# A planned two-layer kernel: seven products for eight in one more pair, and a planner with issue intervals

## The chip, the cores and the metric

The kernel runs on one core of a Trainium2 chip. The metric is the device time of one launch in microseconds: 1023.86 us, the median of three runs (1023.51 to 1023.94). TensorE (PE) does the matmuls, VectorE (DVE) and ScalarE (ACT) everything between them, SyncE (SP) issues nearly all transfers; GpSimd (POOL) does next to nothing. Each engine works through its own list in the order in which the program gives it.

## The reference

From q, k and v of 6016 tokens by 256 channels the reference makes a channel attention, and then two feed-forward layers on 6016 tokens with 2048 hidden features:

```
qn = q / (norm(q over tokens) + 1e-6);  kn likewise
a  = softmax(kn^T @ qn / tau);  x = v @ a              # 6016 x 256
x  = (max(x @ w_in, 0) ** 2) @ w_out                   # layer 1
h  = x @ moe2_w_in
y  = max(0.01 * h, h) @ moe2_w_out                     # layer 2
```

The weights arrive as 64-bit floats and are converted in the kernel.

## The kernel before, in words

A short attention stage (to about 52 us) makes the 256 x 256 softmax, which is folded into layer 1's w_in. Then come the two layers. The tokens are cut into six pairs of two blocks of 512 tokens (448 in pair 4); pairs are counted from 0 in each layer, and a layer's eight groups of 256 hidden features (g = 0 to 7) from 0 too. A unit is one pair and one group, so there are 96 units. Layer 1's pair 0 has a fixed order of its own (PLAIN, line 532); the other 88 units are laid out by a planner.

Every fp32 product is three matmuls on split operands: each operand is a high part and a low part, and mm3 (line 555) adds low x high, high x high and high x low into one bank. "A cast" on ACT makes the high part, "a low" on DVE (line 116) subtracts it to give the low part.

In a unit the first product (x @ w_in) is a 2 x 2 block product done with seven block products in place of eight: F1, F2, F3, F5, F4, F7, F6 in this order (line 907), each three matmuls into two banks. Banks are ha and hb, or hc and he in every second unit of a plain pair. After F1 ACT copies the bank away (C11, line 1317), after F3 it makes copy u, after F4 copy w; DVE adds F2's, F5's and F6's bank to these copies (lines 564 and 566), and F7 is read by ACT (line 1331). F6 may start only when DVE has added F5's bank to copy w. Then ACT squares (layer 1) or applies the leaky relu, casts, and DVE makes the lows.

The second product (g @ w_out) of a unit is either plain, eight block products (line 583, form "P"), or shared, seven products P1 to P7 (line 645, form "S"). Before, form S is used in layer 2's pairs 0 to 4 for the groups SG = 0, 1, 3, 4, 6 (lines 55 and 550). A pair with such groups is called mixed: its units all use banks ha and hb, bank c gathers P1, P6 and P7 (yA in the profile) and bank e gathers P5 (yF). A form-S unit needs four subtractions on DVE (lines 1420 to 1423), three more casts and lows (b), and weight sums S1 to S4 of w_out; the gathered banks are added up by take_shared and combine (lines 1470 and 1547).

Layer 2's weights are converted in 16 steps (Unit, line 130, and convert, line 978) during layer 1's pairs 2 to 5, spread evenly (line 1593).

The planner (line 751 on) makes a list of tasks with an engine, a cost, a due time, dependencies and buffers; one unit of time is a 512-column matmul. simulate (line 804) lets each engine take the ready task with the smallest due time; a result can be used on another engine lat = 0.3 after the task's end. TensorE takes the next first product, or a second product that waits in a list, with small gaps (PE, line 859). The due times are written by hand relative to the unit's start. The plan is made eight times, each on the unit starts of the one before, and the last is used. A function deadlines (line 1621) that works times back from the matmuls stands in the file, but late_start stays None and nothing calls it.

Of the kernel before, what the change touches and what calls it, by code (L numbers as in the profile page):

```python
# [18 lines left out]
P = 128  # L19
# [12 lines left out]
def attn_moe_moe2(  # L32
# [22 lines left out]
    SG = (0, 1, 3, 4, 6)  # L55
# [30 lines left out]
    def bank(tag, name):  # L86
# [43 lines left out]
    class Unit:  # L130


        def __init__(self, kind, L, g):
            self.kind, self.L, self.g = kind, L, g
            self.blocks = L == 2 and (kind == "i" or g in SG)

# [614 lines left out]
    tasks, lines = [], {}  # L751
    COST = {"v": 10, "out": 9, "y": 5, "wi": 2.6, "wo": 1.6, "wst": 2, "store": 2, "x": 1.6}
# [51 lines left out]
    def simulate(pe):  # L804
# [16 lines left out]
        while n:  # L821
# [31 lines left out]
    TURNS = 8  # L853
    LOAD = 22
# [74 lines left out]
    def batch_of(n):  # L929
        i = sorted(SG).index(units[n][2])  # L930
        return i // BATCH, i % BATCH
# [6 lines left out]
    def is_mixed(L, p):  # L938
        return L == 2 and p < NP - 1 and len(SG) > 0
# [6 lines left out]
    def build(base):  # L946
# [31 lines left out]
        def convert(u, due, loaded=None, first=None, pace=4, begin=0):  # L978
# [16 lines left out]
            re = T("ACT", 2.7, d(0.5), u.rebias, deps=[t], uses=[ce])  # L995
# [43 lines left out]
        for n in range(NG):  # L1039
# [3 lines left out]
            if g + 1 < NG:  # L1043
# [7 lines left out]
                lo = [T("DVE", 2.5, at0(m["fold_low"] + 2.6 * i), lambda i=i, pw=pw: fold_low(i, *pw[i]), deps=[hi[i]], uses=[b])  # L1051
                      for i in range(KC)]
# [6 lines left out]
            for i, (half, fb) in enumerate(((0, 0), (0, 1), (1, 0), (1, 1))):  # L1059
# [9 lines left out]
                relus[half, fb] = T("ACT", 2.7, at0(m["relu"][i]), plain_relu, n, half, fb, deps=[t], **k)  # L1069
# [63 lines left out]
        def prepare_x(L, p):  # L1133
# [34 lines left out]
            else:  # L1168
# [4 lines left out]
                t = T("SP", "x", t0 + 30, load, alloc=xr, lat=2.5 * LOAD, deps=[stores["y", 1, p, 0], stores["y", 1, p, 1]])  # L1173
# [83 lines left out]

        def load_wo(n):
            L, p, g = units[n]
            b = wo_b[L, p, g] = Buf("wo", 4, base[n] + 13)  # L1260
            dep = stores["o", L, g]
            if form_of(n) == "P":
                def load():
                    src = wo_d[L, g]
                    if L == 2 and g in SG:
                        src = src[:, :, :4].rearrange("p a (k b) m -> p a k b m", k=KC)
                    nc.sync.dma_start(raw(wo_tile(L, p, g)), src)

                wo_ready[L, p, g] = T("SP", "wo", base[n] + 13, load, alloc=b, lat=LOAD, deps=[dep])
                return  # L1270

            def load():
                t = wo_t[L, p, g] = wpool.tile([P, 2, 4, P], F32R, tag="wo", name="wo", bufs=4)
                nc.sync.dma_start(raw(t), wo_d[L, g][:, :, 1:5])

            def load_s1():
                t = late_w[n, "S1"] = wpool.tile([P, 2, 1, P], F32R, tag="ws", name="ws", bufs=2)
                nc.sync.dma_start(raw(t), wo_d[L, g][:, :, 5:6])

            def load_s23():  # L1280
                t = late_w[n, "S23"] = cpool.tile([P, 2, 2, P], F32R, tag="ce", name="ws")
                nc.sync.dma_start(raw(t), wo_d[L, g][:, :, 6:])
# [187 lines left out]
        def take_shared(p, which, b, after):  # L1470
            w = WIDTH[p]
            s = (w + 32) / 544
            n = (NP + p) * NG
            due = base[n] + (b + 1) * 4 * 42
            a = lambda: y_t[2, p, "A"][:, :w]

            def new():
                if which == "P1":
                    sum_t[p, "P1"] = cpool.tile([P, 512], F32, tag="cm", name="acc")
                elif which == "U":  # L1480
                    t = vpool.tile([P, 2, 512], F32, tag="v", name="acc")
                    sum_t[p, "U"], sum_t[p, "V"] = t[:, 0], t[:, 1]
                nc.scalar.copy(sum_t[p, which][:, :w], a())

            def more():
                add(sum_t[p, which][:, :w], sum_t[p, which][:, :w], a())

            due += {"P1": 0, "U": 30, "V": 45}[which]
            if b == 0:
                if which == "P1":  # L1490
                    sums_b[p, "P1"] = Buf("cm", 2, due)
                elif which == "U":
                    sums_b[p, "U"] = sums_b[p, "V"] = Buf("v", 3, due)
                k = dict(uses=[sums_b[p, which]]) if which == "V" else dict(alloc=sums_b[p, which])
                t = T("ACT", 2.7 * s, due - 20, new, deps=after + ([got["U"]] if which == "V" else []), **k)
            else:
                t = T("DVE", 3 * s, due - 20, more, deps=after + [got[which]], uses=[sums_b[p, which]])
# [5 lines left out]
        def mixed_items(n):  # L1503
            L, p, g = units[n]
            gs = sorted(SG)
            prev = n - 1 if g - 1 in SG else None
# [12 lines left out]
            else:  # L1519
# [5 lines left out]
                if ends:  # L1525
                    members = [m for m in range(n - g, n) if units[m][2] in SG and batch_of(m)[0] == b]
                    take_shared(p, "P1", b, list(in_batch))
                    in_batch.clear()
                    for which, acc, mine in (("P6", "U", own[:3]), ("P7", "V", own[3:])):
# [3 lines left out]
                        take_shared(p, acc, b, xs)  # L1533
# [10 lines left out]
            if g == NG - 1:  # L1544
                combine(p)

        def combine(p):
            w = WIDTH[p]
            s = (w + 32) / 544
            y = lambda half, d: y_t[2, p, half, d][:, :w]  # L1550
            S = lambda which: sum_t[p, which][:, :w]
            f = lambda: y_t[2, p, "F"][:, :w]
            t0 = base[(NP + p + 1) * NG]
            D1 = 3 * s
            B = sums_b
            Y = lambda half, d: done[2, p, half, d]

            def x_new():
                sum_t[p, "X"] = cpool.tile([P, 512], F32, tag="cm", name="acc")
                add(S("X"), S("V"), y(0, 0))  # L1560

            y11 = T("DVE", D1, t0 + 40, lambda: add(S("P1"), S("P1"), y(0, 1)), deps=[got["P1"], *Y(0, 1)], uses=[B[p, "P1"]])
            B[p, "X"] = Buf("cm", 2, t0 + 45)
            y21 = T("DVE", D1, t0 + 45, x_new, deps=[got["V"], *Y(0, 0)], alloc=B[p, "X"], uses=[B[p, "V"]])
            fu = T("DVE", D1, t0 + 42, lambda: add(S("U"), S("U"), f()), deps=[got["U"], *f_done], uses=[B[p, "U"]])
# [104 lines left out]
```

## Time and profile before

| | |
|---|---|
| Median of runs | 1023.86 us (1023.51 to 1023.94) |
| Profiled execution | 1023.25 us |
| Span of the profile | 1021.5 us |
| TensorE busy | 1016.0 us (99%), 4693 matmuls |
| Weight loads (PEld) busy | 859.1 us (84%) |
| VectorE busy | 793.8 us (78%), 1131 instructions |
| ScalarE busy | 765.8 us (75%), 1170 instructions |
| Mean granted TensorE clock | 0.999 |
| Moved by DMA | 215.95 MB, 211 GB/s |

The profile is one execution; 1.75 us of its time lie outside the span. Matmuls overlap, so a group's duration is longer than the distance between starts, and the distance is what counts. In the table by stretches each pair of layers 1 and 2 is one stretch, from the pair's first first-product to the next pair's.

### The profile page before, as it was taken

The numbers are of one execution on the slowest core, as the hardware profiler recorded it, in microseconds if no ns is written. First come the engines' busy times: TensorE is split into PE (matmuls) and PEld (weight loads), VectorE is DVE, ScalarE is ACT, GpSimd is POOL, SyncE is SP. The second block draws the span as 40 slices with busy tenths as digits, with TensorE's granted clock in tenths as the row PEclk, the third lists the DMA queues.
The fourth block names the chain that finished last, engine by engine and source line by source line (L and its number), as shares of the span: only waits on it lengthen the run. The fifth ranks groups of instructions, "written<-read, shape, count | busy, mean of one in ns | idle before, by whom it ended". The sixth has DMA issues, their size and how long they took to land.

```text
span 1021.5 us, 13002 instructions
## 1 busy us (share of the span) xinstructions
PE 1016.0 (99%) x4693; PEld 859.1 (84%) x4693; DVE 793.8 (78%) x1131; ACT 765.8 (75%) x1170; POOL 0.7 (0%) x6
## 2 busy tenths in 40 slices
PE   9999999999999999999999999999999999999998
PEld 8888888888888888998888888888888888898887
DVE  5999878967976977888747779979979979977442
ACT  6798777877877877888767778778777777775662
POOL 0000000000000000000000000000000000000000
PEclk9999999999999999999999999999999999999999
DMA  9795568568678667787735555755755654664521
GB/s 350 278 233 179 165 209 245 177 220 256 235 255 271 226 249 235 270 292 274 271 135 189 197 191 191 221 200 178 220 190 200 199 197 173 199 232 157 173 78 42
DMA packets 125600, 215.95 MB, mean 211 GB/s; under 512 B 49376, under 2 KB 65760, under 8 KB 123232
## 3 DMA queue, kind: packets, MB, share of 16 engines
q1 hardware_dynamic: 124816, 214.46, 62.8%
q8 instruction: 37, 0.61, 0.2%
q10 hardware_dynamic: 720, 0.66, 0.2%
q14 instruction: 27, 0.22, 0.1%
HBM read 174.98 MB, written 40.11 MB: 211 GB/s over the span
## 4 chain that ended last, share of the span: by engine, by line
PE 99%; ACT 0%; DVE 0%; issue 0%
PE y L557 40%; PE ha L557 17%; PE hb L557 13%; PE hc L557 6%; PE yA L557 5%; PE he L557 5%; PE h L714 4%; PE sT L399 4%; PE y L597 2%; PE yF L557 2%; PE pw L265 1%; PE warm L364 0%; ACT e L486 0%; PE pn L373 0%; ACT whl L205 0%; DVE cm L178 0%
## 5 line engine op out<-in xcount | busy, mean ns | idle before, releaser
L557 PE MATMUL y<-g,wo 128*128 128x512 f32 (+1 forms) x1758 | 448.6, 385 | 0.0
L557 PEld LDWEIGHTS y<-g,wo 128*128 128x128 f32 x1758 | 329.8, 188 | 62.1
L116 DVE TENSOR_TENSOR g<-c,g 128x1024 fp32r<-128x1024 f32 (+1 forms) x192 | 229.4, 1200 | 80.3 <-ACT g L684 59.4
L557 PE MATMUL ha<-x,wi 128*128 128x512 f32 (+1 forms) x768 | 212.7, 385 | 0.0
L557 PEld LDWEIGHTS ha<-x,wi 128*128 128x128 f32 x768 | 143.7, 188 | 27.3 <-ACT c L1317 0.5
L557 PE MATMUL hb<-x,wi 128*128 128x512 f32 (+1 forms) x576 | 159.6, 385 | 0.0
L684 ACT CAST g<-c 128x1024 fp32r<-128x1024 f32 (+1 forms) x142 | 145.8, 1034 | 13.2 <-PE y L557 7.6
L557 PEld LDWEIGHTS hb<-x,wi 128*128 128x128 f32 x576 | 107.6, 188 | 20.8 <-ACT c L1324 0.4
L699 ACT ACTIVATE c<-c 128x512 f32<-128x512 f32 (+1 forms) x160 | 98.5, 621 | 18.4 <-DVE c L564 16.1
L557 PE MATMUL hc<-x,wi 128*128 128x512 f32 (+1 forms) x288 | 80.1, 386 | 0.0
L701 ACT ACTIVATE c<-c 128x512 f32<-128x512 f32 (+1 forms) x98 | 60.8, 621 | 12.8 <-DVE c L566 12.1
L1412 DVE TENSOR_TENSOR c<-c 128x512 f32<-128x512 f32 (+1 forms) x100 | 67.7, 677 | 3.1 <-ACT c L701 0.6
L1317 ACT COPY w<-ha 128x512 f32<-128x512 f32 (+1 forms) x64 | 37.0, 578 | 43.7 <-PE ha L557 43.3
L557 PEld LDWEIGHTS hc<-x,wi 128*128 128x128 f32 x288 | 53.7, 188 | 10.6 <-ACT c L1317 0.8
L557 PE MATMUL he<-x,wi 128*128 128x512 f32 (+1 forms) x216 | 60.2, 387 | 0.0
L1390 ACT CAST g<-c 128x1024 fp32r<-128x1024 f32 (+1 forms) x50 | 51.3, 1025 | 4.7 <-DVE c L1412 3.3
L116 DVE TENSOR_TENSOR b<-c,b 128x512 fp32r<-128x512 f32 (+1 forms) x75 | 49.5, 673 | 2.9 <-ACT b L1405 2.3
L1405 ACT CAST b<-c 128x512 fp32r<-128x512 f32 (+1 forms) x75 | 44.5, 610 | 5.7 <-PE yA L557 2.4
L714 PE MATMUL h<-x,wi 128*128 128x512 f32 x192 | 47.9, 391 | 0.0
L116 DVE TENSOR_TENSOR x<-xr,x 128x1024 fp32r<-128x1024 f32 (+3 forms) x44 | 46.9, 1066 | 1.1 <-ACT x L1188 1.0
L557 PEld LDWEIGHTS he<-x,wi 128*128 128x128 f32 x216 | 40.1, 188 | 7.7 <-DVE c L564 0.6
L1317 ACT COPY u<-ha 128x512 f32<-128x512 f32 (+1 forms) x64 | 36.9, 576 | 12.5 <-PE ha L557 9.7
(134 smaller groups left out, 1170.7 us busy)
## 6 DMA issues: line engine op xcount, KB each, us to landing
wi<-wi SPq DMA_DIRECT2D x80, 896.0 KB, 5.1
wo<-wo SPq DMA_DIRECT2D x96, 512.0 KB, 4.7
wi<-wi SPq DMA_DIRECT2D x24, 512.0 KB, 4.1
wst<-in_moe_w_in_dram SPq DMA_DIRECT2D x16, 512.0 KB, 6.4
wst<-in_moe_w_out_dram SPq DMA_DIRECT2D x16, 512.0 KB, 5.7
wi<-wis SPq DMA_DIRECT2D x8, 1024.0 KB, 5.3
ws<-wo SPq DMA_DIRECT2D x25, 256.0 KB, 3.1
x<-o SPq DMA_DIRECT2D x20, 256.0 KB, 5.5
```

What stands on the lines that cost most here:

```text
L116: tt(lo, x, raw(hi), op=ALU.subtract)
L399: nc.tensor.matmul(sT[j][:, :C], t[:, 0, i, j * P : (j + 1) * P], t[:, 1, i], start=n == 0 and i == 0, stop=last_tile and i == g - 1,)
L557: nc.tensor.matmul(ps, a[m], b[n], start=first and i == 0, stop=i == 2, skip_group_check=True)
L597: nc.tensor.matmul(y_bank(L, p, 1, t // 2)[:, t % 2 * C : (t % 2 + 1) * C], gt[:, a, fb, t * P : (t + 1) * P], wo[:, b, :, fb], start=(g, ...
L684: nc.scalar.copy(g_t[n, half][:, 0, :, :w], c)
L699: nc.scalar.activation(c, c, AF.Square)
L701: nc.scalar.activation(c, c, AF.Prelu, alpha=0.01)
L714: nc.tensor.matmul(h_t[n, half, fb][:, :w], a[i], b[j], start=start, stop=stop, skip_group_check=True)
L1317: nc.scalar.copy(to, h(0))
L1390: nc.scalar.copy(g_t[n, name][:, 0, :, :w], result(n, half, w))
L1405: nc.scalar.copy(b_t[n, name][:, 0, :w], c(half, fb))
L1412: tt(c(*to), c(*a), c(*b), op=ALU.subtract)
```

## The change

Form S is no longer tied to layer 2. A table GROUPS gives the groups for each layer and pair: layer 1's pair 5 gets 0, 1, 3, 4, 6, and layer 2's pairs 0 to 4 get 0, 2, 3, 4, 6 where they had 0, 1, 3, 4, 6. For layer 1 the weight sums of w_out are made once: in pair 4, when a group's plain weights are loaded, wo_sums joins high and low, makes the four sums, splits them and stores them to wo_s, from which pair 5 loads. combine for layer 1 stores the four sums to x2 straight from its accumulators. Layer 2's conversions are spread over pairs 2 to 4 (CONV_BEGIN, CONV_END).

The planner changes too. A task's cost on DVE and ACT is now the distance to the next start, 0.37 and 0.45 less than before, and its result comes 0.6 and 0.65 after that; a result of TensorE comes 0.95 after its cost, before 0.3. From the third plan on, tasks of DVE and ACT are ordered by deadlines(), worked back from the matmuls that need them, and of the plans from the third on the one whose TensorE ends first is used.

```diff
-    SG = (0, 1, 3, 4, 6)
+    GROUPS = {(1, 5): (0, 1, 3, 4, 6), **{(2, p): (0, 2, 3, 4, 6) for p in range(5)}}
+    SG = {L: sorted({g for (l, _), x in GROUPS.items() if l == L for g in x}) for L in (1, 2)}
...
-        return "S" if L == 2 and p < NP - 1 and g in SG else "P"
+        return "S" if g in GROUPS.get((L, p), ()) else "P"
...
+    PIPE = {"DVE": (0.37, 0.6), "ACT": (0.45, 0.65), "PE": (0, 0.95), "POOL": (0, 0.6)}
...
+            else:
+                less, lat = PIPE[engine]
+                cost -= less
...
-        known = {t: sorted((b.due, b.due + 30) for b in lines.get(t, ())) for t in free_lines}
+        known = {t: sorted((b.due, b.due + 60) for b in lines.get(t, ())) for t in free_lines}
...
+    FIRST_MIXED = min([p for L, p in GROUPS if L == 1], default=0)
+    CONV_BEGIN, CONV_END = 2, 5
...
+        def wo_sums(n, ready, b):
...
+            def join():
+                r["x"] = cpool.tile([P, 8, P], F32, tag="whl", name="wr")
+                r["s"] = out_sums(r["x"])
+                hi, lo = (raw(wo_t[L, p, g][:, m]).rearrange("p k b m -> p (k b) m") for m in range(2))
+                tt(r["x"][:, :4], hi, lo, op=ALU.add)
...
+            t = T("DVE", 3, e, join, deps=[ready], alloc=xb, uses=[b])
+            for i in range(4):
+                t = T("DVE", 1.1, e + 1, lambda i=i: r["s"][i](), deps=[t], uses=[xb])
+            wb = Buf("wis", 1, e + 6)
+            t = T("ACT", 4.6, e + 6, high, deps=[t], alloc=wb, uses=[xb])
+            t = T("DVE", 5.2, e + 12, lows, deps=[t], uses=[xb, wb])
+            stores["o", 1, g, "s"] = T("SP", "store", e + 20, store, deps=[t], uses=[wb])
...
+                if L == 1 and g in SG[1] and p == FIRST_MIXED - 1:
+                    wo_sums(n, wo_ready[L, p, g], b)
...
+                if L == 1:
+                    for which, d, dep in parts:
+
+                        def put_sum(which=which, d=d, half=half):
+                            nc.sync.dma_start(x2_d[p][:, SLOT[d, half], :w], S(which))
...
-                span = base[6 * NG] - 60 - base[2 * NG]
+                begin = base[int(CONV_BEGIN * NG)] + 60
+                span = base[int(CONV_END * NG)] - 60 - begin
...
+        if turn >= 2 and (best is None or free["PE"] < best[0] - 0.05):
+            best = free["PE"], list(tasks), dict(c_tag)
+        if turn >= 1:
+            late_start = deadlines()
+    tasks[:] = best[1]
```

How the order moves is seen at two places. On TensorE, in layer 1's pair 5 before, one unit (x_3434, x_3885, x_3803 and x_3792 are the four tiles of the pair's x; F1, F2, F3, F5, F4, F7, F6 are the ha and hb rows, in this order, and the y rows are second products):

```order
L557 MATMUL ha<-x_3434,wi 128x512 x3
L557 MATMUL hb<-x_3792,wi 128x512 x3
L557 MATMUL y<-g,wo 128x512 x3
L557 MATMUL ha<-x_3885,wi 128x512 x3
L557 MATMUL y<-g,wo 128x512 x3
L557 MATMUL hb<-x_3803,wi 128x512 x3
L557 MATMUL ha<-x_3803,wi 128x512 x3
L557 MATMUL y<-g,wo 128x512 x6
L557 MATMUL ha<-x_3885,wi 128x512 x3
L557 MATMUL hb<-x_3792,wi 128x512 x3
L557 MATMUL y<-g,wo 128x512 x12
```

The same pair on TensorE now, one unit (x_3493, x_3965, x_3906, x_3899 are the same four tiles):

```order
L559 MATMUL ha<-x_3493,wi 128x512 x3
L559 MATMUL hb<-x_3899,wi 128x512 x3
L559 MATMUL y<-g,wo 128x512 x3
L559 MATMUL ha<-x_3965,wi 128x512 x3
L559 MATMUL y<-b,wo 128x512 x3
L559 MATMUL hb<-x_3906,wi 128x512 x3
L559 MATMUL yF<-g,ws 128x512 x3
L559 MATMUL ha<-x_3906,wi 128x512 x3
L559 MATMUL y<-g,wo 128x512 x3
L559 MATMUL yF<-g,ws 128x512 x3
L559 MATMUL ha<-x_3965,wi 128x512 x3
L559 MATMUL hb<-x_3899,wi 128x512 x3
```

Products of the shared form (y<-b, yF, and yA outside these rows) stand among the first products; from F4 (the third ha row) to F6 (the last hb row) there are nine matmuls in both.

On VectorE, the start of layer 1's pair 5 before (c<-c,hb and the like are the adds on the banks, g<-c,g are lows; ce, cm and wr belong to the conversion of layer 2's weights):

```order
L564 ISA c<-c,hb 128x512
L116 TENSOR_TENSOR g<-c,g 128x2x448
L149 TENSOR_SCALAR ce<-wst 128x512
L156 TENSOR_SCALAR cm<-wst 128x512
L159 SCALAR_TENSOR_TENSOR cm<-wst,cm 128x512
L162 SCALAR_TENSOR_TENSOR ce<-wst,ce 128x512
L564 ISA c<-w,hb 128x512
L174 SCALAR_TENSOR_TENSOR wr<-cm,ce 128x256 x2
L220 TENSOR_TENSOR wr<-wr 128x128
L221 TENSOR_TENSOR wr<-wr 128x128
L564 ISA c<-u,hb 128x512
```

VectorE at that place now (L1456 c<-c are the four subtractions of a shared unit, b<-c,b its lows):

```order
L566 ISA c<-w,hb 128x512
L566 ISA c<-u,hb 128x512
L118 TENSOR_TENSOR g<-c,g 128x1024
L1456 TENSOR_TENSOR c<-c 128x512
L566 ISA c<-c,hb 128x512
L118 TENSOR_TENSOR b<-c,b 128x512
L1456 TENSOR_TENSOR c<-c 128x512 x3
L118 TENSOR_TENSOR b<-c,b 128x512 x2
L566 ISA c<-w,hb 128x512
L750 COPY o<-y 128x448
L118 TENSOR_TENSOR g<-c,g 128x1024
```

The conversion's rows have left the pair, and the subtractions and extra lows of the shared form have come.

## Rows read from the trace of the kernel before

**Rows 1.** The page: busy time by engine, and the chain that ended last.
```profile
PE 1016.0 (99%) x4693; PEld 859.1 (84%) x4693; DVE 793.8 (78%) x1131; ACT 765.8 (75%) x1170; POOL 0.7 (0%) x6
...
PE 99%; ACT 0%; DVE 0%; issue 0%
```

**Rows 2.** Timeline of TensorE, 560 to 568 us: start, duration, instructions, count.
```profile
560.80 0.84 PE L557 MATMUL hb<-x,wi 128*128 128x512 f32 x3
...
567.60 0.85 PE L557 MATMUL y<-g,wo 128*128 128x512 f32 x3
```

**Rows 3.** Stretches (layer 1's pairs 0, 2 to 5; layer 2's pair 0): busy us.
```profile
60.00:143.00 83.00, 83.00 (x401) 69.99 (x400) 75.98 (x126) 68.81 (x101) 0.00 (x0) 1.00 0.65 200
...
220.50:302.70 82.20, 82.20 (x362) 67.32 (x362) 65.12 (x97) 64.41 (x95) 0.00 (x0) 1.00 0.75 251
302.70:384.50 81.80, 81.80 (x362) 67.23 (x361) 61.12 (x92) 62.16 (x94) 0.00 (x0) 1.00 0.74 250
384.50:459.00 74.50, 74.50 (x362) 67.33 (x361) 61.34 (x92) 59.32 (x97) 0.00 (x0) 1.00 0.78 269
459.00:539.70 80.70, 80.70 (x362) 67.55 (x361) 55.35 (x77) 61.41 (x93) 0.00 (x0) 1.00 0.61 222
539.70:617.30 77.60, 77.60 (x344) 64.21 (x343) 57.98 (x75) 59.20 (x94) 0.00 (x0) 1.00 0.54 192
```

**Rows 4.** Waits of TensorE's weight loads: total us, times, longest us.
```profile
PEld hc L557 <- ACT c L1317: 0.8, 4, 0.2
PEld he L557 <- DVE c L564: 0.6, 3, 0.3
PEld ha L557 <- ACT c L1317: 0.5, 2, 0.3
```

**Rows 5.** Timeline, 882 to 884 us (PEld is the weight load).
```profile
882.06 0.77 PE L557 MATMUL hb<-x,wi 128*128 128x448 f32 x3
...
882.67 0.77 PE L557 MATMUL ha<-x,wi 128*128 128x448 f32 x3
...
882.87 0.55 ACT L1324 ACTIVATE c<-hb 128x448 f32<-128x448 f32 x1 [0.39 <-PE hb L557]
...
883.47 0.50 PEld L557 LDWEIGHTS hb<-x,wi 128*128 128x128 f32 x3 [0.40 <-ACT c L1324]
883.47 0.87 PE L557 MATMUL hb<-x,wi 128*128 128x448 f32 x3
```

**Rows 6.** Groups of VectorE by line and shape: count, busy us, mean ns, idle before.
```profile
L116 DVE TENSOR_TENSOR g<-c,g 128x1024 fp32r<-128x1024 f32 x160 | 194.7, 1222 | 68.0 <-ACT g L684 51.1 <-ACT g L1390 15.8
L1412 DVE TENSOR_TENSOR c<-c 128x512 f32<-128x512 f32 x80 | 55.2, 690 | 2.0
L116 DVE TENSOR_TENSOR b<-c,b 128x512 fp32r<-128x512 f32 x60 | 40.6, 687 | 2.7 <-ACT b L1405 2.3
...
L116 DVE TENSOR_TENSOR wis<-wr,wis 128x1024 fp32r<-128x1024 f32 x13 | 15.8, 1217 | 0.3 <-ACT wis L205 0.3
...
L220 DVE TENSOR_TENSOR wr<-wr 128x128 f32<-128x128 f32 x21 | 6.0, 288 | 0.3
...
L1230 DVE TENSOR_TENSOR wr<-wi 128x512 f32<-128x512 f32 x8 | 5.5, 685 | 0.0
```

**Rows 7.** Groups of ScalarE by line and shape.
```profile
L1405 ACT CAST b<-c 128x512 fp32r<-128x512 f32 x60 | 36.3, 621 | 4.8 <-PE yA L557 2.1 <-PE y L557 0.8 <-ACT c L701 0.3
...
L1317 ACT COPY w<-ha 128x512 f32<-128x512 f32 x52 | 30.6, 588 | 38.8 <-PE ha L557 38.7
```

**Rows 8.** The page's DMA issues: count, KB each, median us to landing.
```profile
wi<-wi SPq DMA_DIRECT2D x80, 896.0 KB, 5.1
```

**Rows 9.** Timeline of VectorE, 862.7 to 864 us.
```profile
862.69 0.62 DVE L566 TENSOR_TENSOR c<-u,hb 128x448 f32<-128x448 f32 x1 [1.16 <-PE hb L557]
863.26 1.09 DVE L116 TENSOR_TENSOR g<-c,g 128x896 fp32r<-128x896 f32 x1
```

**Rows 10.** Waits of all engines: total us, times, longest us.
```profile
DVE c L564 <- ACT w L1317: 27.4, 24, 3.1
```

More of the change, by code (lines that the diff above doesn't have):

```diff
@@ L134, in __init__ @@
             self.kind, self.L, self.g = kind, L, g
-            self.blocks = L == 2 and (kind == "i" or g in SG)
+            self.blocks = L == 2 and (kind == "i" or g in SG[2])
         def load(self):
@@ L938, in is_mixed @@
     def is_mixed(L, p):
-        return L == 2 and p < NP - 1 and len(SG) > 0
+        return len(GROUPS.get((L, p), ())) > 0
     c_tag = {}
@@ L1260, in load_wo @@
             b = wo_b[L, p, g] = Buf("wo", 4, base[n] + 13)
-            dep = stores["o", L, g]
+            dep = stores["o", L, g] if L == 2 or form_of(n) == "P" else stores["o", 1, g, "s"]
+            sums_d = wo_d[L, g] if L == 2 else wo_s.get(g)
             if form_of(n) == "P":
@@ L1490, in take_shared @@
                 if which == "P1":
[L1491 removed]
+                    sums_b[L, p, "P1"] = Buf("cm", 2, due)
                 elif which == "U":
[L1493 to L1494 removed]
+                    sums_b[L, p, "U"] = sums_b[L, p, "V"] = Buf("v", 3, due)
+                k = dict(uses=[sums_b[L, p, which]]) if which == "V" else dict(alloc=sums_b[L, p, which])
                 t = T("ACT", 2.7 * s, due - 20, new, deps=after + ([got["U"]] if which == "V" else []), **k)
             else:
[L1497 removed]
+                t = T("DVE", 3 * s, due - 20, more, deps=after + [got[which]], uses=[sums_b[L, p, which]])
             got[which] = t
@@ L1525, in mixed_items @@
                 if ends:
-                    members = [m for m in range(n - g, n) if units[m][2] in SG and batch_of(m)[0] == b]
-                    take_shared(p, "P1", b, list(in_batch))
+                    members = [m for m in range(n - g, n) if units[m][2] in gs and batch_of(m)[0] == b]
+                    take_shared(L, p, "P1", b, list(in_batch))
                     in_batch.clear()
@@ L1554, in combine @@
             D1 = 3 * s
             B = sums_b
-            Y = lambda half, d: done[2, p, half, d]
+            Y = lambda half, d: done[L, p, half, d]
             def x_new():
-                sum_t[p, "X"] = cpool.tile([P, 512], F32, tag="cm", name="acc")
+                sum_t[L, p, "X"] = cpool.tile([P, 512], F32, tag="cm", name="acc")
                 add(S("X"), S("V"), y(0, 0))
-            y11 = T("DVE", D1, t0 + 40, lambda: add(S("P1"), S("P1"), y(0, 1)), deps=[got["P1"], *Y(0, 1)], uses=[B[p, "P1"]])
@@ L1569, in combine @@
+            fv = T("DVE", D1, t0 + 50, lambda: add(S("V"), S("V"), f()), deps=[got["V"], y21, *f_done], uses=[B[L, p, "V"]])
+            y12 = T("DVE", D1, t0 + 53, lambda: add(S("U"), S("U"), y(1, 1)), deps=[fu, *Y(1, 1)], uses=[B[L, p, "U"]])
+            y22 = T("DVE", D1, t0 + 56, lambda: add(S("V"), S("V"), y(1, 0)), deps=[fv, *Y(1, 0)], uses=[B[L, p, "V"]])
             F_after[0] = [fu, fv]
-            if p == NP - 2:
+            q = (L, p + 1) if p < NP - 1 else (2, 0)
+            if not is_mixed(*q):
```

95 lines of the change are left out of this document (56 added, 39 removed).

## The prediction

> **What bounds the kernel now.** I read the engine table and the chain of waits first, then the table by stretches cut at the pairs, then TensorE's timeline, then its waits. TensorE is busy 1016.0 of 1021.5 us and the chain that ended last is TensorE for 99% [rows 1]. Busy time of a pipelined engine proves little, so the issue rate has to be looked at: in the first mixed pair of layer 2 ten groups of three matmuls start between 560.80 and 567.60 us, 30 matmuls in 6.80 us, or 0.2267 us each, without one skipped beat [rows 2]. Cut at the pairs, TensorE fills every stretch, while VectorE fills 69 to 92% of it and never runs out [rows 3]. So the time is the number of matmuls times their issue interval, plus the places where a weight load had to wait. After the first fold those places are few: three groups of waits with nine places and 1.9 us [rows 4], and a tenth place of 0.40 us [rows 5], 2.3 us together. Not all of that reaches the matmuls. At that tenth, at 883.47 us, the weight load waited 0.40 us for ScalarE; the matmul group before began at 882.67 and, at the 0.61 us that a group of 448 columns took just before (882.06 to 882.67), the next was due at 883.28 and began at 883.47, so 0.19 us was lost [rows 5]. Half of 2.3 us, about 1.1 us, is my estimate of all that better ordering could still give back there.
>
> **The matmuls removed.** In the last pair of layer 1 (pair 5; a layer's pairs count from 0) five of eight groups now take seven products of three matmuls for the second product in place of eight. That is 5 x 3 = 15 matmuls of 512 columns; the order of TensorE has 15 fewer in all, so nothing else is added there (layer 2 only takes group 2 for group 1, five groups as before). 15 x 0.2267 = 3.40 us, all of it on the engine that sets the end. The Trainium skill, TensorE: Matmul & The Clock Gate (section Wait — 56ns, not 53.3ns?), gives 215.7 ns for a warm matmul of 512 columns; by it the term would be 3.24 us. The row has 226.7 ns, and the row decides.
>
> **What VectorE and ScalarE get.** For each of the five groups VectorE makes four subtractions of 0.690 us and three lows of 0.687 us (the two lows of 1.222 us stay). The pair adds twelve sums of product banks, priced at the 0.685 us of a 512-column add, and drops two copies of the same shape [rows 6]: 20 x 0.690 + 15 x 0.687 + 10 x 0.685 = 31.0 us. The weight sums for these groups, made once in pair 4, are a join of 0.685, four block sums of 0.288 and a low of 1.217 us [rows 6]: 3.05 us, five times, 15.3 us. The conversion of layer 2's weights is spread over three pairs, not four. By the order, pairs 2, 3 and 4 of layer 1 get 16, 25 and 15 more of these preparing instructions, the sums among them, and pair 5 has 26 fewer. At 3.05 / 6 = 0.51 us each, VectorE goes in pair 2 from 65.1 to 73 of 82.2 us, in pair 3 from 61.1 to 74 of 81.8, in pair 4 from 61.3 to 69 of 74.5, which is 93%. Pair 5 and the first pair of layer 2, into which its last sums run over, go together from 113.3 to 113.3 - 13.3 + 31.0 = 131 of 155 us, 85% [rows 3]. The nearest row to a pair this full is the first one, with VectorE at 76.0 of 83.0 us (92%) and TensorE at 83.0 of 83.0 [rows 3]. So I cost these additions at nothing; the cover is VectorE's idle time, and were pair 4 pushed past its 74.5 us, each further microsecond would be one of span. ScalarE gets 15 casts of 0.62 us and a few more [rows 7], some 16 us in two pairs where it is busy 61.4 of 80.7 and 59.2 of 77.6 us [rows 3].
>
> **Transfers.** Five stores of 1 MB and, net, ten smaller loads more pass SP's queue, and the conversion's loads come earlier. By the shapes in the order pair 4 goes from 20 to 23 MB. It moved 269 GB/s there at a DMA share of 0.78 [rows 3], so about 0.90 after. The wi loads land 5.1 us after their issue [rows 8] and are issued two groups, some 20 us, ahead: a transfer half as slow again stays hidden. I cost it at nothing.
>
> **The new order.** The planner now gives VectorE and ScalarE 0.37 and 0.45 of a matmul (84 and 102 ns) less per instruction and lets a result come later than the next start. The trace supports that direction: a VectorE add of 0.62 us began at 862.69 and the next instruction at 863.26, 0.57 later [rows 9]. It also counts 0.95 of a matmul, not 0.3, from TensorE to a reader: the group that began at 882.06 should have issued its last column by 882.67 and ScalarE began at 882.87, 0.20 us or 0.9 of a matmul later [rows 5]. These are truer numbers, but a plan that counts slack exactly also leaves less of it, and every place of the old waits moves. From below, all 1.1 us of the old waits go. From above, VectorE's work in pair 5 is not covered at all, since the order there is wholly new: 31 us. These ends are far apart; the nearest row, the 92% pair with TensorE full, speaks for the low end. I take two more waits of the size seen at 883.47, 2 x 0.2 = 0.4 us, one for each of the two fullest new stretches (pairs 4 and 5).
>
> **Sum.** The profiled execution took 1023.25 us: 1021.5 of span and 1.75 around it. 1023.25 - 3.40 + 0.4 = 1020.25 us. The median of the runs, 1023.86, lies 0.61 above the profiled one, so 1020.86 us; I forecast 1020.8.
>
> **Rivals.** (a) The gain is eaten by small waits. For: the orders of VectorE and ScalarE change everywhere, not in one pair, and there are 88 groups with several round trips each. Against: the tightest round trip keeps its distance in the order, nine matmuls from the product that the copy w reads to the one that the sum over it releases, before and after. Fourteen waits of 0.2 us give 2.8 us: 1023.86 - 3.40 + 2.8 = 1023.3 us, no change.
>
> (b) Slower: VectorE's queue order blocks that round trip. From the product to the copy 0.20 us [rows 5], the copy 0.588 [rows 7], the add 0.690, as another VectorE operation of that shape [rows 6], together 1.48 of the 9 x 0.2267 = 2.04 us there are; 0.56 is left, less the hops. If the planner lets a low of 1.222 us begin just before the copy is done, the add starts up to 1.17 us late (the low less the 0.05 of overlap [rows 9]), and TensorE stands 0.6 us. Before, VectorE stood idle for this copy at 24 places of layer 1's relu adds alone, for 27.4 us [rows 10]; a fuller VectorE has less of that idle time. The change is slower by more than 0.2% once 3.40 + 2.05 = 5.45 us are lost, from ten such groups of 88 on; at thirteen the time is 1023.86 - 3.40 + 7.8 = 1028.3 us. Against: a plan that knows the intervals can see such a low coming, and the first pair, with VectorE at 92%, shows no such loss [rows 3].
>
> (c) The issue intervals are wrong. The Trainium skill, VectorE: DVE Perf Modes (section The DRAIN you can't avoid), says that the next VectorE instruction does not start until the pipe has emptied. As a mechanism of this kernel: if the next start waited for the result, the planner's 84 ns would not exist; the 107 VectorE instructions in pair 4 (92 by the row and 15 more [rows 3]) would need 107 x 0.05 = 5.4 us more, 74.4 of 74.5 us, and the pair would begin to set the pace; with a loss of the 3.4 us that was gained the time is 1023.9 us. Rows 9 show the next start ahead of the result, so this has 1 in 100.
>
> (d) The change doesn't remove what it says: closed by the order's 15 fewer matmuls.
>
> **How the numbers follow.** A measurement of this kernel can tell about 0.2%, 2 us, from no change. The forecast, from 1019.0 (old waits gone, no new ones, the median's offset kept: 1023.86 - 3.40 - 1.1 = 1019.4, and 0.4 for the spread of the runs) to 1021.8 us: 0.63, all of it faster. Rival (a) and (c), 1021.8 to 1025.9: 0.25, no change. Rival (b): 0.12, slower. The likeliest case's own range is 1019.0 to 1021.8. The range for 8 in 10 leaves out the upper part of (b) and the far ends: 1018.9 to 1025.5 us.
>
> **What would show it.** Right: TensorE's rows give 15 fewer matmuls of 512 columns, starts still 0.2267 us apart in pair 5, its length near 78 us, VectorE in pair 4 of layer 1 near 93% with TensorE full, and the waits of weight loads for VectorE and ScalarE after the first fold still under 4 us in all. Rival (a) shows as many more such waits, of 0.1 to 0.4 us, spread over all pairs; rival (b) as waits of hb and he loads for the sum over w (line 564 and 566 before), of half a microsecond and more, with a low of line 116 in front on VectorE. A loss in one pair alone, with the DMA share there near 1, would be the transfers and would make the step on them wrong.

## The result: 1.4% slower, with 73 waits of TensorE's weight loads

The changed kernel takes 1037.62 us, the median of four runs (1036.97 to 1038.54), against 1023.84 us (1023.51 to 1023.94) before: a ratio of 1.0136, with a 95% interval of 1.0118 to 1.0153. The forecast was 1020.8 us with a range up to 1025.5; neither held, nor did the direction. The profiled execution took 1036.97 us with a span of 1035.2 us, 13.7 us more than the span before.

The page of the changed kernel, engine by engine and the chain that ended last:

```profile
PE 1026.4 (99%) x4678; PEld 850.3 (82%) x4678; DVE 829.8 (80%) x1206; ACT 776.7 (75%) x1191; POOL 0.7 (0%) x6
...
PE 79%; DVE 11%; ACT 6%; issue 2%; DMA 2%; ACTq 0%; SPq 0%; DVEq 0%
```

The 15 matmuls are gone (4678 for 4693). TensorE still counts as busy for 99%, as in [rows 1], so that number says nothing here. The chain says it: it was TensorE for 99% and is TensorE for 79%, with VectorE in 11% and ScalarE in 6% of it. And 15 matmuls fewer are busy 10.4 us longer, since a matmul's tail, which else lies beside the next one, fills a gap in that count.

The table by stretches, cut at the pairs of the changed kernel (start and end, length, then busy us and instructions of TensorE, weight loads, VectorE, ScalarE, GpSimd, the granted clock, DMA share and GB/s): layer 1's pairs 0, 2, 3, 4 and 5, layer 2's pairs 0 and 3.

```profile
60.00:143.07 83.07, 82.96 (x399) 69.75 (x398) 77.06 (x129) 68.12 (x101) 0.00 (x0) 1.00 0.65 206
...
223.84:307.95 84.11, 83.99 (x362) 66.65 (x360) 72.89 (x113) 67.39 (x100) 0.00 (x0) 1.00 0.80 269
307.95:391.34 83.39, 83.08 (x361) 66.95 (x360) 71.16 (x117) 65.72 (x99) 0.00 (x0) 1.00 0.85 285
391.34:467.77 76.43, 75.94 (x361) 66.66 (x360) 66.00 (x107) 60.67 (x98) 0.00 (x0) 1.00 0.87 297
467.77:545.50 77.73, 77.44 (x341) 63.06 (x339) 63.03 (x84) 62.90 (x101) 0.00 (x0) 1.00 0.59 203
545.50:625.44 79.94, 79.94 (x349) 64.71 (x348) 66.09 (x89) 61.13 (x97) 0.00 (x0) 1.00 0.57 196
...
785.28:865.01 79.73, 79.55 (x347) 64.08 (x345) 67.23 (x91) 59.77 (x95) 0.00 (x0) 1.00 0.60 197
```

The same view of the kernel before for layer 2's pair 3, which the rows ahead of the prediction did not need:

```profile
773.84:852.04 78.20, 78.20 (x346) 64.75 (x345) 67.14 (x90) 60.11 (x95) 0.00 (x0) 1.00 0.61 200
```

Beside [rows 3]: pair 0, whose order is fixed by hand, is as long as it was, with VectorE at 93%. The planned pairs are longer: pairs 2, 3 and 4 of layer 1 by 1.9, 1.6 and 1.9 us with the same matmuls. Layer 2's pair 3, in which only one group's number changed and VectorE has the same 67 us of work, is 1.5 us longer. Pair 5 of layer 1 is 3.0 us shorter, but its stretch has 21 matmuls fewer (341 for 362): the 15, and six that now stand behind its last cut (the next stretch has 349 for 344). 21 x 0.2267 = 4.8 us, so pair 5 too loses some 1.8 us. The loss goes with the planner, then, and not with the work, the DMA share or VectorE's fill. TensorE's clock is 1.00 (2.4 GHz) throughout.

Where the weight loads wait in the changed kernel (waiting engine, tile and line, the tile and line that releases it: total us, times, longest us):

```profile
PEld hb L559 <- DVE c L566: 4.7, 11, 0.9
PEld ha L559 <- ACT c L1361: 4.2, 12, 0.5
PEld hb L559 <- DVE c L568: 4.0, 11, 0.7
PEld ha L559 <- ACT u L1361: 2.5, 7, 0.6
PEld hb L559 <- ACT hb L1361: 2.4, 9, 0.5
PEld he L559 <- DVE c L566: 1.9, 5, 0.7
...
PEld ha L559 <- ACT w L1361: 1.4, 4, 0.6
```

All lines of this view for line 559 give 26.1 us in 73 places (the view lists waits of more than 0.15 us). VectorE's adds end 27 of them, 10.6 us, and ScalarE's copies and activations 46, 15.5 us. The same lines of the kernel before give 2.9 us in 13 places: the ten of [rows 4] and [rows 5] and three more of 0.2 us. Not all of a weight load's wait is lost, since loads run ahead of matmuls (at 663.50 below, the load waits 0.73 us and the matmuls come 0.47 late). Counted on the matmuls themselves (from start to start, less the undisturbed distance of 227 ns, or 200 ns for 448 columns), TensorE loses 4.7 us after the first 60 us in the kernel before and 22.1 us in the changed one. So the balance is 22.1 - 4.7 = 17.4 us of new waits, less 3.4 us for the matmuls: 14.0 us, where the spans differ by 13.7.

**What such a wait on VectorE looks like.** The timeline of the changed kernel in layer 2's pair 1 (start, duration, instructions; in brackets the idle time before and who ended it):

```profile
656.24 1.22 DVE L118 TENSOR_TENSOR g<-c,g 128x1024 fp32r<-128x1024 f32 x1
...
657.50 1.49 DVE L1456 TENSOR_TENSOR c<-c 128x512 f32<-128x512 f32 x2
...
657.65 0.62 ACT L1449 CAST b<-c 128x512 fp32r<-128x512 f32 x1
...
658.90 0.68 DVE L118 TENSOR_TENSOR b<-c,b 128x512 fp32r<-128x512 f32 x1
...
659.62 1.42 DVE L1456 TENSOR_TENSOR c<-c 128x512 f32<-128x512 f32 x2
...
660.96 1.29 DVE L118 TENSOR_TENSOR b<-c,b 128x512 fp32r<-128x512 f32 x2
...
661.18 0.59 ACT L1361 COPY w<-ha 128x512 f32<-128x512 f32 x1 [0.21 <-PE ha L559]
...
662.16 0.69 DVE L1205 TENSOR_TENSOR xr<-xr 128x512 f32<-128x512 f32 x1
662.35 0.84 PE L559 MATMUL ha<-x,wi 128*128 128x512 f32 x3
662.76 0.68 DVE L568 TENSOR_TENSOR c<-w,hb 128x512 f32<-128x512 f32 x1
...
663.50 0.53 PEld L559 LDWEIGHTS hb<-x,wi 128*128 128x128 f32 x3 [0.73 <-DVE c L568]
663.50 0.98 PE L559 MATMUL hb<-x,wi 128*128 128x512 f32 x3 [0.30 <-DVE c L568]
...
664.32 0.86 PE L559 MATMUL y<-g,wo 128*128 128x512 f32 x3
```

The matmul group before began at 662.35 and has three matmuls, so the next was due at 662.35 + 3 x 0.2267 = 663.03. It began at 663.50, 0.47 us late, since VectorE added over copy w only from 662.76. The copy had been ready at 661.77. VectorE was not idle: from 656.24 on it went through nine other instructions with pauses of 0.03 to 0.10 us.

Those nine took 662.76 - 656.24 = 6.52 us. The planner's numbers for them (a low of 1024 columns 5.4 - 0.37 units, a 512-column operation 3 - 0.37) are 5.03 + 8 x 2.63 = 26.07 units of 0.2267 us, 5.91 us. By its own reckoning the add would have begun at 662.15 and ended some 0.2 us before TensorE needed it. The missing 0.61 us stands in the distances between starts. From the single subtraction of x at 662.16 to the add at 662.76, which does not read it, it is 0.60 us, the planned size. Three starts wait for VectorE's own instruction before them and come 0.03 to 0.04 us behind its end: the first subtraction at 657.50, which overwrites what the low of 656.24 reads; the third at 659.62, 0.72 us after the low of 658.90, whose input it overwrites; and the fourth at 660.35 (659.62 + 1.42 - 0.69), 0.73 us after the third, whose result it reads. They are 0.12, 0.12 and 0.13 us later than planned, 0.37 us together. The second subtraction, at 658.30 (657.50 + 1.49 - 0.69), is 0.20 us later: it starts 0.03 us behind the end of ScalarE's cast (657.65 + 0.62 = 658.27), which reads the same buffer, and the list of tasks does not make it wait for that cast. The last 0.04 us are spread over the other five. So more than half of the delay is VectorE waiting for itself, and a third is a wait for ScalarE that the plan does not have.

The greater part, in the code, is one line of simulate: a dependency is counted with its delay on another engine, but on its own engine as met at x.end. Until the change x.end was the end of the operation. Now it is the next start, 84 to 102 ns ahead of it.

**And on ScalarE.** The timeline of the changed kernel in layer 1's pair 1:

```profile
169.03 0.63 ACT L701 ACTIVATE c<-c 128x512 f32<-128x512 f32 x1 [1.23 <-DVE c L566]
...
169.34 0.86 PE L559 MATMUL hb<-x,wi 128*128 128x512 f32 x3
...
169.56 0.57 ACT L1361 COPY u<-ha 128x512 f32<-128x512 f32 x1
...
170.18 0.53 PEld L559 LDWEIGHTS ha<-x,wi 128*128 128x128 f32 x3 [0.41 <-ACT u L1361]
170.18 0.96 PE L559 MATMUL ha<-x,wi 128*128 128x512 f32 x3
```

The ha group was due at 169.34 + 0.68 = 170.02 and began at 170.18, behind copy u. In ScalarE's list an activation stands in front of the copy, and this one had waited until 169.03 for an add of VectorE. So a delay on one engine is handed on by the other. In 72 of the 73 places the instruction that ended the wait had started at most 0.06 us behind the end of the one before it on its engine, so it stood behind other work in that engine's list.

### The profile page after: what moved, and what is told of

It reads as the page before. It is cut to its first block, busy times and chain, and to the rows that moved or that the text cites. A ratio compares the mean times of both kernels' runs of the same rounds, so it can differ in the third digit from the quotient of the medians.

```text
span 1035.2 us, 13116 instructions
## 1 busy us (share of the span) xinstructions
PE 1026.4 (99%) x4678; PEld 850.3 (82%) x4678; DVE 829.8 (80%) x1206; ACT 776.7 (75%) x1191; POOL 0.7 (0%) x6
## 4 chain that ended last, share of the span: by engine, by line
PE 79%; DVE 11%; ACT 6%; issue 2%; DMA 2%; ACTq 0%; SPq 0%; DVEq 0%
PE y L559 29%; PE ha L559 15%; PE hb L559 12%; PE yA L559 5%; PE hc L559 5%; PE he L559 3%; PE sT L401 2%; PE h L716 2%; PE y L599 2%; DVE g L118 2%; PE yF L559 2%; ACT g L686 2%; ACT c L701 1%; DVE c L1456 1%; DMA qk<-in_k_dram 1%
## 5 line engine op out<-in xcount | busy, mean ns | idle before, releaser
L559 PE MATMUL y<-g,wo 128*128 128x512 f32 (+1 forms) x1668 | 429.8, 386 | 0.0
L559 PEld LDWEIGHTS y<-g,wo 128*128 128x128 f32 x1668 | 313.1, 188 | 59.3
L559 PE MATMUL ha<-x,wi 128*128 128x512 f32 (+1 forms) x816 | 229.1, 389 | 0.7 <-ACT w L1361 0.2
L559 PE MATMUL hb<-x,wi 128*128 128x512 f32 (+1 forms) x612 | 173.1, 391 | 1.6 <-DVE c L566 0.8
L1456 DVE TENSOR_TENSOR c<-c 128x512 f32<-128x512 f32 (+1 forms) x120 | 81.5, 680 | 4.1
L118 DVE TENSOR_TENSOR b<-c,b 128x512 fp32r<-128x512 f32 (+1 forms) x90 | 59.1, 676 | 13.7 <-ACT b L1449 13.2
L559 PE MATMUL hc<-x,wi 128*128 128x512 f32 (+1 forms) x240 | 67.3, 389 | 0.2
L559 PEld LDWEIGHTS hc<-x,wi 128*128 128x128 f32 x240 | 44.3, 188 | 10.9 <-ACT c L1361 1.5
L559 PE MATMUL he<-x,wi 128*128 128x512 f32 (+1 forms) x180 | 50.5, 389 | 0.2 <-DVE c L566 0.2
L559 PE MATMUL yA<-b,ws 128*128 128x512 f32 (+1 forms) x180 | 48.0, 386 | 0.0
```

The costliest lines, as they stand in the source:

```text
L118: tt(lo, x, raw(hi), op=ALU.subtract)
L559: nc.tensor.matmul(ps, a[m], b[n], start=first and i == 0, stop=i == 2, skip_group_check=True)
L1456: tt(c(*to), c(*a), c(*b), op=ALU.subtract)
```

## Experiments

Each kernel is the changed one with the edit shown, timed in three rounds beside the kernel before on the same chip. Ratios are to the kernel before, with 95% intervals. The kernel before took 1023.44 to 1024.24 us beside them, so a difference between two versions that were not timed together is good to some 0.8 us. "Waits" are those of the weight loads for line 559, as above. The letters D, C and W are explained in the first expectation.

### The work with the plan of before, and the plan with the work of before

```diff
-    PIPE = {"DVE": (0.37, 0.6), "ACT": (0.45, 0.65), "PE": (0, 0.95), "POOL": (0, 0.6)}
+    PIPE = {"DVE": (0, 0.3), "ACT": (0, 0.3), "PE": (0, 0.3), "POOL": (0, 0.3)}
...
-        if turn >= 2 and (best is None or free["PE"] < best[0] - 0.05):
+        if turn == TURNS - 1:
             best = free["PE"], list(tasks), dict(c_tag)
-        if turn >= 1:
-            late_start = deadlines()
```

> The changed kernel's work (seven products in layer 1's pair 5, its weight sums, the conversion in three pairs, layer 2's groups 0, 2, 3, 4, 6) laid out by the planner as it was: old costs, 0.3 to every reader, due times written by hand, the last plan. Theory D (the order by latest starts makes the waits) and theory C (the shorter costs make them) both expect the forecast's saving: 1023.8 - 3.4 = 1020.4 us, 1019 to 1022. Theory W (the added work itself fills VectorE until TensorE waits) expects most of the loss to stay, 1034 to 1038 us, with the waits in layer 1's pairs 2 to 5.

1021.08 us, ratio 0.9968 (0.9955 to 0.9981), waits of 3.3 us in 8 places. (Of the planner's changes only the 60 in place of 30 where buffers are chosen is left in.) The new work alone is worth the 3.2 us by which 1021.08 lies under the 1024.24 of the kernel before in that job. The additions on VectorE and ScalarE and the transfers cost nothing that can be seen.

```diff
-    GROUPS = {(1, 5): (0, 1, 3, 4, 6), **{(2, p): (0, 2, 3, 4, 6) for p in range(5)}}
-    SG = {L: sorted({g for (l, _), x in GROUPS.items() if l == L for g in x}) for L in (1, 2)}
+    GROUPS = {(2, p): (0, 1, 3, 4, 6) for p in range(5)}
+    SG = {1: [], 2: [0, 1, 3, 4, 6]}
...
-    CONV_BEGIN, CONV_END = 2, 5
+    CONV_BEGIN, CONV_END = 2, 6
```

> The work of the kernel before (no seven products in layer 1, groups 0, 1, 3, 4, 6, conversion over four pairs) laid out by the new planner as a whole. D and C expect what the planner cost in the changed kernel, some 17 us over before: 1038 to 1043 us. W expects before's time, 1022 to 1026 us.

1044.64 us, ratio 1.0200 (1.0183 to 1.0218), waits of 31.1 us in 86 places: 1.6 us above what D and C expected. The work of before, with VectorE's 1131 instructions, loses 20 us under the new planner. The loss is the planner's alone.

### The latest starts, or the costs

```diff
-        if turn >= 1:
-            late_start = deadlines()
```

> The changed kernel with the due times written by hand in place of latest starts; the shorter costs, the longer way from TensorE and the choice of the best plan stay. D expects the waits gone: 1019 to 1023 us. C expects them to stay: 1034 to 1039 us. W expects 1034 to 1038 us.

1038.02 us, ratio 1.0136 (1.0121 to 1.0151), waits of 26.4 us in 70 places. Without the order by latest starts nothing changes, so with the new costs the order by latest starts neither harms nor helps, and D is out.

```diff
-    PIPE = {"DVE": (0.37, 0.6), "ACT": (0.45, 0.65), "PE": (0, 0.95), "POOL": (0, 0.6)}
+    PIPE = {"DVE": (0, 0.3), "ACT": (0, 0.3), "PE": (0, 0.3), "POOL": (0, 0.3)}
```

> The changed kernel with the old costs (nothing taken off, 0.3 to every reader) and with the order by latest starts. C expects the waits gone: 1019 to 1023 us. D expects them to stay or grow, since the latest starts come from less true numbers: 1033 to 1045 us. W expects 1034 to 1038 us.

1020.39 us, ratio 0.9962 (0.9947 to 0.9977): under both kernels, with an interval that leaves out 1, and 17.2 us under the changed one by one line of numbers. This is the version to keep. It cannot be told from the first experiment, which has the same costs and no latest starts. Its page and its waits of line 559:

```profile
PE 1012.0 (99%) x4678; PEld 856.6 (84%) x4678; DVE 832.5 (82%) x1206; ACT 780.2 (77%) x1191; POOL 0.7 (0%) x6
...
PE 97%; DMA 2%; ACT 1%; DVE 0%; SPq 0%; issue 0%; DVEq 0%; ACTq 0%
```

```profile
PEld hc L559 <- ACT w L1361: 1.0, 1, 1.0
...
PEld ha L559 <- ACT c L1361: 0.4, 2, 0.2
PEld hc L559 <- ACT c L1361: 0.4, 2, 0.2
PEld hb L559 <- DVE c L566: 0.2, 1, 0.2
```

VectorE has the same 1206 instructions and is the fuller of the two (82% for 80%), in a shorter span, and TensorE has six waits left. How the order differs is seen in VectorE's timeline of this kernel, the same unit as at 656.24 above:

```profile
644.24 1.22 DVE L118 TENSOR_TENSOR g<-c,g 128x1024 fp32r<-128x1024 f32 x1
645.57 1.49 DVE L1456 TENSOR_TENSOR c<-c 128x512 f32<-128x512 f32 x2
646.97 0.69 DVE L118 TENSOR_TENSOR b<-c,b 128x512 fp32r<-128x512 f32 x1
647.69 1.42 DVE L1456 TENSOR_TENSOR c<-c 128x512 f32<-128x512 f32 x2
649.03 0.70 DVE L629 STREAM_TRANSPOSE o<-acc 128x512 f32<-128x512 f32 x1
649.70 0.69 DVE L568 TENSOR_TENSOR c<-w,hb 128x512 f32<-128x512 f32 x1
650.30 0.68 DVE L118 TENSOR_TENSOR b<-c,b 128x512 fp32r<-128x512 f32 x1
```

From the low at 644.24 to the add at 649.70 it is 5.46 us; the old costs for these seven instructions (5.4 + 5 x 3, and 3.1 for the transpose) are 23.5 units, 5.33 us, 0.13 us too few where the new ones were 0.61 too few. And one operation stands between the last subtraction and the add, where the changed kernel has three. simulate does not look ahead: a free engine takes what is ready. With 2.63 units for each operation the planner's VectorE was through with the subtractions early and filled the time until copy w with three more; with 3 units it had time for one. Neither number is right for both cases: 2.63 units are 0.60 us, 3 units 0.68, and a start that waits for its own engine comes after 0.72.

### An engine's own results, or the reserve

Two readings of the shorter costs remained: that own results are used too early (the text calls it S), or that the costs had held a reserve that is gone (M).

```diff
-                    d.ready = max(d.ready, x.end + (0 if d.engine == e and x.lat < 1 else x.lat))
+                    d.ready = max(d.ready, x.end + x.lat)
```

> The changed kernel with one thing altered: an instruction that reads a result of its own engine counts as ready when that result is there (0.6 or 0.65 after the cost on VectorE and ScalarE), not at the next start. Theory S (the planner lets an engine's own results be used at once, while the trace shows 176 VectorE and 139 ScalarE starts some 34 ns after the result they wait for, where others start 80 to 100 ns ahead of it) expects most of the 17 us to go: 1020 to 1026 us. Theory M (the old, too high cost of every instruction was a reserve, and without it long operations stand in front of the add that TensorE waits for) expects little: 1032 to 1039 us.

1023.67 us, ratio 1.0003 (0.9993 to 1.0013), waits of 5.5 us in 26 places. Making own results wait as well takes back 13.9 of the 17.2 us. In this trace 89 starts on VectorE and 87 on ScalarE, after the first 60 us, come some 0.03 us behind the same engine's last end, where the changed kernel has 176 and 139. The waits that are left are short (weight loads, as above):

```profile
PEld he L559 <- DVE c L566: 0.9, 4, 0.3
PEld hb L559 <- ACT hb L1361: 0.9, 5, 0.2
PEld ha L559 <- ACT c L1375: 0.7, 4, 0.2
PEld hb L559 <- DVE c L568: 0.7, 3, 0.3
```

### One engine at a time

```diff
-    PIPE = {"DVE": (0.37, 0.6), "ACT": (0.45, 0.65), "PE": (0, 0.95), "POOL": (0, 0.6)}
+    PIPE = {"DVE": (0, 0.3), "ACT": (0.45, 0.65), "PE": (0, 0.95), "POOL": (0, 0.6)}
```

> The changed kernel with VectorE's old cost (nothing taken off, 0.3 to a reader); ScalarE keeps 0.45 and 0.65, TensorE 0.95. If the missing time is VectorE's: 1019 to 1024 us. If ScalarE's: 1032 to 1038 us. If both count alike: 1026 to 1031 us.

1025.72 us, ratio 1.0023 (1.0014 to 1.0033), waits of 9.2 us in 26 places, 1.7 us above what was expected if the time was VectorE's; the longest groups are now for ScalarE.

```diff
-    PIPE = {"DVE": (0.37, 0.6), "ACT": (0.45, 0.65), "PE": (0, 0.95), "POOL": (0, 0.6)}
+    PIPE = {"DVE": (0.37, 0.6), "ACT": (0, 0.3), "PE": (0, 0.95), "POOL": (0, 0.6)}
```

> The changed kernel with ScalarE's old cost; VectorE keeps 0.37 and 0.6, TensorE 0.95. If the missing time is VectorE's: 1032 to 1038 us. If ScalarE's: 1019 to 1024 us. If both count alike: 1026 to 1031 us.

1028.43 us, ratio 1.0051 (1.0035 to 1.0067), waits of 14.3 us in 40 places, most for VectorE's adds. Either engine's costs alone take back more than half (11.9 and 9.2 us), together 21.1, where both at once, TensorE's 0.95 kept, take back 14.8 (the next run). So the loss is not divided between the engines; many of the waits go when either of them is planned with room.

```diff
-    PIPE = {"DVE": (0.37, 0.6), "ACT": (0.45, 0.65), "PE": (0, 0.95), "POOL": (0, 0.6)}
+    PIPE = {"DVE": (0, 0.3), "ACT": (0, 0.3), "PE": (0, 0.95), "POOL": (0, 0.6)}
```

> The changed kernel with the old costs of VectorE and ScalarE and with TensorE's new 0.95 to a reader. Theories S and M both put the loss on the engines' costs, not on this number: 1018 to 1021.5 us, as with all old costs (1020.4). If the longer way from TensorE makes waits by itself: over 1024 us.

1022.84 us, ratio 0.9993 (0.9984 to 1.0003), waits of 3.7 us in five places. Beyond what was expected by 1.3 us: with the old costs, the longer delay of TensorE's results costs 2.4 us (1022.84 against 1020.39 with 0.3).

### How much is reserve

Each of these four has own results delayed by the edit of simulate above, and this line of costs beside it:

```diff
-    PIPE = {"DVE": (0.37, 0.6), "ACT": (0.45, 0.65), "PE": (0, 0.95), "POOL": (0, 0.6)}
+    PIPE = {"DVE": (0.37, 0.6), "ACT": (0.45, 0.65), "PE": (0, 0.3), "POOL": (0, 0.6)}
```

> As result_chain (own results counted when they are there), and TensorE's way to a reader back at 0.3. result_chain left 3.3 us to the 1020.4 of all old costs, and pe_lat_only showed 2.4 us for the 0.95 by itself. If the 0.95 explains the rest: 1020 to 1022 us. If the rest is the lost reserve in the engines' costs (theory M): 1023 to 1027 us, since a reader of TensorE is now planned too early as well.

1027.92 us, ratio 1.0042 (1.0028 to 1.0056), waits of 14.0 us in 38 places; both expectations failed. With exact costs on the other engines the true 0.95 is worth 4.3 us; without it the kernel is slower than before.

```diff
-    PIPE = {"DVE": (0.37, 0.6), "ACT": (0.45, 0.65), "PE": (0, 0.95), "POOL": (0, 0.6)}
+    PIPE = {"DVE": (0, 0.3), "ACT": (0, 0.3), "PE": (0, 0.3), "POOL": (0, 0.3)}
```

> All old costs, and own results counted 0.3 after the cost. By theory S the old costs came out right since a cost of 3 covers the 720 ns to an own result nearly (680 ns); 40 ns more per dependent start takes away the last error: 1019 to 1021 us, at or a little under 1020.4. If more reserve makes the plan worse: over 1022 us.

1022.82 us, ratio 0.9990 (0.9980 to 0.9999). Old costs and a delay on top are 2.4 us worse than old costs alone, which S had not expected: too much caution costs as well, if little.

```diff
-    PIPE = {"DVE": (0.37, 0.6), "ACT": (0.45, 0.65), "PE": (0, 0.95), "POOL": (0, 0.6)}
+    PIPE = {"DVE": (0.185, 0.415), "ACT": (0.225, 0.425), "PE": (0, 0.3), "POOL": (0, 0.6)}
```

> Own results counted when they are there, TensorE's way at 0.3, and half of the old reserve put back into the costs of VectorE and ScalarE (the next start 42 and 51 ns later than the trace has it, the result when the trace has it). Theory M: better than chain_pe_03 by 1 us or more, 1019.5 to 1021.5 us. Theory S alone: the same as chain_pe_03 within 0.7 us.

1021.10 us, ratio 0.9973 (0.9962 to 0.9983), waits of 2.1 us in four places. Half of the old reserve per instruction, with every result's time unchanged, is worth 6.8 us against 1027.92. S alone would have left the time as it was, so M holds too.

```diff
-    PIPE = {"DVE": (0.37, 0.6), "ACT": (0.45, 0.65), "PE": (0, 0.95), "POOL": (0, 0.6)}
+    PIPE = {"DVE": (0.185, 0.415), "ACT": (0.225, 0.425), "PE": (0, 0.95), "POOL": (0, 0.6)}
```

> As half_reserve, with TensorE's way to a reader at the 0.95 that the trace has in place of 0.3. chain_pe_03 against result_chain put 4.3 us on this number when the costs are exact, pe_lat_only against old_costs put it 2.4 us the other way when they carry the full reserve. If the true number is always the better one: 1018.5 to 1020.5 us, the fastest version. If half a reserve already covers it: 1020.3 to 1022 us, the same as half_reserve (1021.1). If the number only spoils plans with a reserve: over 1022.5 us.

1021.70 us, ratio 0.9984 (0.9974 to 0.9994): not told apart from 0.3. Once some reserve is there, the delay of TensorE's results decides nothing.

## Why the prediction was wrong

**What held.** The term of 15 x 0.2267 = 3.40 us: the new work with the old plan measured 3.2 us. The terms of zero for VectorE, ScalarE and the transfers held as well. Pair 4 came to 297 GB/s at a DMA share of 0.87, where about 0.90 was estimated. VectorE's fill there is 66.0 of 76.4 us, 86% where 93% was estimated, because the preparing work came out smaller (107 records as counted on, 66.0 us for 69). At such fills the old costs lose nothing: from 384 to 458 us of that version VectorE is busy 65.4 of 74.0 us, and the whole takes 1020.39 us.

**The step that failed** is the one headed "The new order". It took + 0.4 us for two more waits; it measured + 17.2 to 17.4 us. I tested the new numbers where they were meant to be true, on one pair of starts [rows 9], found 0.57 us, and from there on treated the plan as one that knows the chip. I asked whether the next start may come ahead of the result, and not whether the code lets the next instruction use that result then. Rows 9 is an independent pair: the low there does not read the add just before it. The dependent ones stood in the same trace: the 80 subtractions with 2.0 us of idle time before them [rows 6] are for the most part starts that waited for their own engine. A count of the starts some 0.03 us behind the same engine's last result, after the first 60 us, and with 0.12 us each on VectorE and 0.13 on ScalarE, would have been 144 x 0.12 + 123 x 0.13 = 33 us of engine time that the new numbers leave out, against the 1.1 us that I let better ordering gain. That number was a warning and not a price: the version with old costs has 151 and 139 such starts and waits in six places; its plan gives a 512-column operation 0.68 us where such a start comes after 0.72. The prediction also read [rows 4] as all of the old waits; the view has 13, not ten, and 2.9 us for 2.3, which moves its 1.1 us by 0.3.

The Trainium skill, VectorE: DVE Perf Modes (section The DRAIN you can't avoid), says that the pipe's emptying does not make a same-engine read after write safe, and that a semaphore between the two is one of the things that do. No run here leaves such a wait out; the rows above show what it costs: 0.03 us behind the result at 660.35, which is read, 0.08 us ahead of one that isn't read at 662.76. I had drawn on that section for rival (c) and judged it on the independent start alone. (c)'s mechanism, a start that waits for the end of the one before, holds in these rows for instructions that depend on their own engine's last one, and only for those. Rival (c) got a chance of 1 in 100.

**The rivals.** What happened is (a)'s picture, small waits over all pairs, with (b)'s cause, other work in front of the instruction that TensorE waits for, on ScalarE more often than on VectorE. I priced (a) at 14 waits, there are 60 more; (b) at 13 groups of 88. "The first pair, with VectorE at 92%, shows no such loss" was no evidence against either: that pair has an order fixed by hand and stayed at 83.07 us in the changed kernel. (b)'s picture as predicted is there too. The timeline of the changed kernel in layer 1's pair 4:

```profile
433.61 1.22 DVE L118 TENSOR_TENSOR wis<-wr,wis 128x1024 fp32r<-128x1024 f32 x1
...
435.68 2.35 DVE L118 TENSOR_TENSOR x<-xr,x 128x1024 fp32r<-128x1024 f32 x2
435.88 0.53 ACT L1361 COPY w<-ha 128x448 f32<-128x448 f32 x1 [0.61 <-PE ha L559]
...
437.50 0.78 PE L559 MATMUL y<-g,wo 128*128 128x448 f32 x3
...
437.95 0.61 DVE L566 CUSTOM_DVE_ANT_0 c<-w,hb 128x448 f32<-128x448 f32 x1
...
438.62 0.50 PEld L559 LDWEIGHTS hb<-x,wi 128*128 128x128 f32 x3 [0.72 <-DVE c L566]
438.62 0.88 PE L559 MATMUL hb<-x,wi 128*128 128x448 f32 x3 [0.34 <-DVE c L566]
```

Copy w is ready at 436.41, two lows of 1.17 us stand in front of the add until 437.95, and the group due at 437.50 + 0.61 = 438.11 begins at 438.62. Here too the planner's clock runs short: the low at 433.61, four sums of 128 columns behind it and the two lows are planned at 4.83 (5.2 - 0.37), 4 x 0.73 (1.1 - 0.37) and 2 x 4.83, 17.4 units or 3.95 us, and took 4.34.

**The size of a wait.** At 883.47 us of the kernel before I counted 0.19 us lost [rows 5]. The group after it shows the rest: the first matmul behind such a wait holds the next one up as well. In the rows above, 663.50 to 664.32 is 0.82 us for three matmuls that take 0.68, and 0.47 + 0.14 = 0.61 us are lost at that one wait.

**What stays open.** The two causes can't be divided cleanly: delaying own results takes back 13.9 us where TensorE's delay is 0.95, and half a reserve 6.8 us where it is 0.3, and each plan is another list. Why the 0.95 gains 4.3 us with exact costs and loses 2.4 with the old ones was not found; in the second case the waits are few and longer. That dependent starts make up most of one delay is shown at the unit above, with a wait for ScalarE as the rest; how often such waits for the other engine, which delaying own results does not mend, play a part was not counted. That most of the 73 waits have this cause is argued from the experiment with delayed own results.

## What to carry to other kernels

A planner's number for an instruction has to be read twice from the trace, once where the next instruction is independent and once where it needs the result, and the code has to be read for which of the two it uses for which. A cost that looks too high may be the reserve that keeps an in-order engine from being packed in front of a result that the bounding engine waits for: before making it exact, look for what pays for delays that the plan does not know. That an engine is under 90% busy protects nothing if the order puts long work in front of a short, urgent instruction; the evidence for or against that has to come from a stretch that the same planner lays out.

## What the runs showed of the hardware

- On VectorE a 512-column instruction starts 0.60 us after the one before it if it does not read its result, and 0.73 us if it does (662.16 to 662.76, and 659.62 to 660.35). One that overwrites what the former reads waits as long (658.90 to 659.62). On ScalarE, over the same trace, independent starts lie about 0.10 us ahead of the former's end and dependent ones 0.03 us behind it.
- A weight load that is late costs TensorE its gap and some 0.1 us more: the matmul behind the wait is followed after about 0.34 us, not 0.227 (the median over the 62 waits of the changed kernel in front of 512 columns). So by an estimate from this ten waits of 0.1 us cost about twice what they show.
- A DMA share of 0.87 over a whole pair (297 GB/s) did no harm: the version with old costs has 0.88 (312 GB/s) from 384 to 458 us, and ran at 1020.39 us.
